# Cosine attention and token/channel mixer on one core: the first pair's loads, its k in two halves, and the sums of the second pair

## The chip, the core and the metric

The kernel runs on one core of one Trainium2 chip. The metric is the device time of one execution in microseconds (us). The engines are named as in the profile: PE (matrix multiplication), DVE (vector), ACT (scalar functions), POOL (general), SP (here it only issues DMAs). PEld is PE's loading of the stationary operand, and a "q" behind a name (SPq, ACTq, POOLq) is that engine's instruction queue when it issues DMAs.

## The reference

Eight batches, twelve heads, 448 tokens, head size 64; the mixer has d_model 768, d_tok 256 and d_ch 1536.

```python
q_n = q / (norm(q, axis=-1) + 1e-6)
k_n = k / (norm(k, axis=-1) + 1e-6)
scores = q_n @ k_n.T / tau                   # per batch and head
attn = softmax(scores)
x = (attn @ v)  as (batch, 448, 768)
h = relu(x.T @ w_tok1) @ w_tok2              # mixes the 448 tokens
u = x + h.T
out = u + relu(u @ w_ch1) @ w_ch2            # mixes the 768 channels
```

## The kernel before

**The unit of work is a pair of heads.** Twelve heads make NPAIR = 6 pairs a batch, and the 48 pairs of all batches are numbered i = 0 to 47. The 448 tokens lie as 112 partitions with 4 chunks each (SC = 112, NCH = 4), so a tile of q, k or v of a pair is 112 x 512 numbers in fp32, 224 KB, and each partition's part of one head is one contiguous run.

**The steps of a pair**, with the helper that records each one. `load_qk` and `load_v` issue the loads: q and v from SP's queue, k of pairs 0 to 2 from ACT's (L101 to L137). `square` squares q (a = 1) or k (a = 0), on ACT or POOL. `sums` adds up the squares over the head size, on DVE (L263). `norms` takes the square root as Ln and Exp on ACT (L276, L277), and, called again with `dve=True`, adds epsilon and takes the reciprocal on DVE (L273, L274). `scale` multiplies q or k by that, with a cast to fp16 into `kq` (L292), q on DVE and k on POOL for the first pairs. `tpose` turns the scaled chunks on PE into the PSUM tile `pst` and copies them on DVE to `qk` (L316, L318). `score(i, c)` multiplies chunk c of k with all of q on PE (L339), and ACT takes the exponential into `pt` (L340). `pv_wide` and `pv` multiply by v, which `cast_v` has cast on POOL (L216). `tok1` and `tok2` are the token mixer; `tok2` needs w_tok2 in the order that `place_w2` (POOL, L188) makes out of `w2n`, which `weights_tok2` loads from POOL's queue (L185). The channel mixer (`m_ch1`, L449, and `m_ch2`, L465) runs batch by batch behind it, as units from a queue that are put between the steps of later pairs.

**The order is written out by hand.** Under `tc.manual_schedule()` every engine runs its instructions in the order in which the helpers are called, and waits where an operand isn't there yet. Ahead of the loop stands a prologue for pairs 0 to 2 (L528 to L581), then a loop over i = 1 to 5 without the channel mixer, one written-out step for i = 6, and the loop for i = 7 to 47 with the channel mixer's units between the steps. In the loop's step i = 1 POOL runs `scale(2, 0)`, `cast_v(1)`, `square(4, 0)` and then `place_w2`, and step i = 2 begins with both scalings of pair 3 on POOL.

**DMA completions** are counted on eight semaphores that SP's and ACT's DMAs take in turn; a DMA that takes a semaphore again waits in its queue until the DMA eight places earlier has landed. SP's queue runs far ahead in this way. Its load of v of pair 4 also waits for `cast_v(0)`, since there are four buffers for v.

**Filler.** `warm(n)` records n matmuls of the identity that nobody reads (L330): 40 at the start, 3 and 5 around the turning of pair 0, later 8, 6 and 10.

Of the kernel before, what the change touches and what calls it, by code (L numbers as in the profile page):

```python
# [7 lines left out]
FP32 = mybir.dt.float32  # L8
FP16 = mybir.dt.float16
AF = mybir.ActivationFunctionType  # L10
ALU = mybir.AluOpType
AXX = mybir.AxisListType

ACT_SET_LN_EXP = 6


def _bcast_free(ap: bass.AP, n: int) -> bass.AP:
    new_ap = list(ap.ap) + [[0, n]]
    return bass.AP(tensor=ap.tensor, offset=ap.offset, ap=new_ap)
# [3 lines left out]
def kernel(  # L23
# [12 lines left out]
    nc = tc.nc  # L36

    B, H, S, E = q.shape
# [3 lines left out]
    SC = 112  # L42
    NCH = S // SC
# [22 lines left out]
    QS = 2 * NCH  # L66
# [17 lines left out]
    qkv = ctx.enter_context(tc.tile_pool(name="qkv", bufs=7))  # L84
# [4 lines left out]
    ps = ctx.enter_context(tc.tile_pool(name="ps", bufs=2, space=bass.MemoryType.PSUM))  # L89
    ps2 = ctx.enter_context(tc.tile_pool(name="ps2", bufs=3, space=bass.MemoryType.PSUM))  # L90

    half = {}
    pipe = {}
# [3 lines left out]

    def old(i):
        return i < OLD

    def load_rows(i, nm, src, bufs):  # L101
        h0 = 2 * (i % NPAIR)
        if old(i):
            t = qkv.tile([SC, QS, E], FP32, name=f"{nm}f_{i}", tag=f"{nm}f", bufs=bufs)
            (nc.scalar if nm == "k" and i < 3 else nc.sync).dma_start(
                out=t[:].rearrange("p (g c) e -> p g (c e)", g=2),
                in_=src[h0:h0 + 2].rearrange("g (p c) e -> p g (c e)", c=NCH))
            return t
        t = qkv.tile([128, 2 * KC, E], FP32, name=f"{nm}f_{i}", tag=f"{nm}f", bufs=bufs)
        nc.sync.dma_start(out=t[:].rearrange("p (g c) e -> p g (c e)", g=2),  # L110
                          in_=src[h0:h0 + 2, 0:128 * KC].rearrange("g (p c) e -> p g (c e)", c=KC))
        return t
# [9 lines left out]
    def load_qk(i):  # L122
        b, h0 = i // NPAIR, 2 * (i % NPAIR)
        n = i // HP
        half.setdefault(n, {})
        st = pipe[i] = {}
        st["q"] = qkv.tile([SC, QS, E], FP32, name=f"qf_{i}", tag="qf")
        nc.sync.dma_start(out=st["q"][:].rearrange("p (g c) e -> p g (c e)", g=2),
                          in_=q[b, h0:h0 + 2].rearrange("g (p c) e -> p g (c e)", c=NCH))
        st["k"] = load_rows(i, "k", k[b], 7)  # L130
        if not old(i) and "kr" not in half[n]:
            half[n]["kr"] = load_rest(i, "k", k[b])
# [51 lines left out]
    def weights_tok2():  # L184
        nc.gpsimd.dma_start(out=w2n[:], in_=moe_w_tok2.rearrange("(tt p) s -> p tt s", p=128))  # L185
# [16 lines left out]
    kqs = [cst.tile([128, 2, NCH, 2, E], FP16, name=f"kq{i}") for i in range(4)]  # L202
# [20 lines left out]
    def lay(i):  # L223
        n = QS if old(i) else KS
        return (slice(0, n), slice(n, n + QS)), (SC if old(i) else 128, SC)
# [25 lines left out]
    def sums_of(i):  # L251
        n, col, w = (-1 - i, 0, 1) if i < SINGLE else (i // HP, i % HP, HP)
        h = half.setdefault(n, {})
        if "ssq" not in h:
            tag = "" if w > 1 else "1"
            h["ssq"] = nrm.tile([128, w, 2 * QS], FP32, name=f"ssq_{i}", tag="ssq" + tag, bufs=4)
            h["rn"] = nrm.tile([128, w, 2 * QS], FP32, name=f"rn_{i}", tag="rn" + tag, bufs=4)
        return h, col

    def sums(i, a0=0, a1=2):  # L260
        n, sl = some(i, a0, a1)
        h, col = sums_of(i)
        nc.vector.tensor_reduce(out=h["ssq"][0:n, col, sl], in_=pipe[i]["sq"][0:n, sl],  # L263
                                axis=AXX.X, op=ALU.add)

    def norms(i0, i1, a0=0, a1=2, dve=False, act=False):
        h, col = sums_of(i0)
        n, sl = some(i0, a0, a1)
        ssq = h["ssq"][0:n, col:col + i1 - i0, sl]
        rn = h["rn"][0:n, col:col + i1 - i0, sl]  # L270
        ne = nes[i0 % 3][0:n, sl]
        if dve:
            nc.vector.tensor_reduce(out=rn[:, 0], in_=ne, axis=AXX.X, op=ALU.add)  # L273
            nc.vector.reciprocal(out=rn, in_=rn)  # L274
            return
        nc.scalar.activation(out=rn, in_=ssq, func=AF.Ln, bias=tiny[0:n])  # L276
        nc.scalar.activation(out=rn if act else ne[:, :, 0], in_=rn if act else rn[:, 0], func=AF.Exp, scale=0.5)  # L277
        if act:
            nc.scalar.activation(out=rn, in_=rn, func=AF.Ln, bias=eps[0:n])
            nc.scalar.activation(out=rn, in_=rn, func=AF.Exp, scale=-1.0)  # L280

    def scale(i, a, eng=None):
        st = pipe[i]
        eng = eng or nc.gpsimd
        sl, np_ = lay(i)
        if "kq16" not in st:
            st["kq16"] = kqs[i % 4]
        kq, p = st["kq16"], np_[a]
        h, col = sums_of(i)
        rn = h["rn"][:, col, sl[a]]  # L290
        n = KC if a == 0 and not old(i) else NCH
        eng.tensor_tensor(out=kq[0:p, a, 0:n].rearrange("p c g e -> p g c e"),  # L292
                          in0=st["kq"[a]][:].rearrange("p (g c) e -> p g c e", g=2),
                          in1=_bcast_free(rn[0:p, 0:2 * n].rearrange("p (g c) -> p g c", g=2), E), op=ALU.mult)
        if n == KC:
            if i < OLD + 4:
                eng.memset(kq[:, 0, KC].rearrange("p g e -> p (g e)"), 0.0)
            for g in range(2):
                p = slice(64 * g, 64 * g + 64)
                eng.tensor_scalar(out=kq[p, 0, KC, g], in0=half[i // HP]["kr"][p, i % HP],  # L300
                                  scalar1=rn[p, 2 * KC:KS], scalar2=1.0, op0=ALU.mult, op1=ALU.mult)
# [2 lines left out]
        scale(i, 0)  # L304
        scale(i, 1)

    def tpose(i, a0=0, a1=2):
        st = pipe[i]
        n = SC if old(i) else 128
        if "qk" not in st:  # L310
            qk = att.tile([128, 2 * NCH * 128], FP16, name=f"qk_{i}", tag="qk")
            st["qk"] = qk[:, 0:2 * NCH * n].rearrange("p (a c s) -> p a c s", a=2, c=NCH)
        pst = ps.tile([128, a1 - a0, NCH, n], FP16, name=f"pst_{i}_{a0}", tag="b")
        for a in range(a0, a1):
            for c in range(NCH):
                nc.tensor.transpose(pst[:, a - a0, c, :], st["kq16"][:n, a, c].rearrange("p g e -> p (g e)"),  # L316
                                    id16[:n, :n])
        nc.vector.tensor_copy(out=st["qk"][:, a0:a1], in_=pst[:])  # L318

    def tpose_dma(i):  # L320
        st = pipe[i]
# [5 lines left out]
    def warm(n, wide=False):  # L327
        w = (ps2 if wide else ps).tile([128, 128], FP32, name=f"warm{len(pipe)}_{n}", tag="s" if wide else "b")
        for _ in range(n):
            nc.tensor.matmul(w[:], id16[:], id16[:], start=True, stop=True)  # L330

    def score(i, c):
        n = SC if old(i) else 128
        qk = pipe[i]["qk"].rearrange("p a c s -> p (a c s)")
        qm = pipe[i]["qk"][:, 1, :, 0:SC]
        psS = ps2.tile([128, 2, 512], FP32, name=f"psS_{i}_{c}", tag="s")
        for hh in range(2):
            hb = slice(hh * 64, hh * 64 + 64)
            nc.tensor.matmul(psS[:, hh, 0:S], qk[hb, c * n:c * n + 128], qm[hb], start=True, stop=True)  # L339
        nc.scalar.activation(out=pts[i % 2][0:n, 2 * S * c:2 * S * (c + 1)].rearrange("p (h s) -> p h s", h=2),  # L340
                             in_=psS[0:n, :, 0:S], func=AF.Exp, scale=inv_tau)
# [183 lines left out]
    SU_AT = {15: [18, 19]}  # L525

    with tc.manual_schedule():
        for i in range(3):  # L528
            load_qk(i)
        load_v(0)  # L530
        load_qk(3)
        load_v(1)
# [1 line left out]
        load_v(2)  # L534
        load_qk(5)
        load_v(3)
        nc.scalar.add_instruction(mybir.InstLoadActFuncSet(
            name=nc.get_next_instruction_name(), act_func_set_id=ACT_SET_LN_EXP,
            ins=[], outs=[]))
        weights_tok1()  # L540

        square(0, 1, act=True)
# [1 line left out]
        sums(0, 1, 2)  # L544
        norms(0, 1, 1, 2)
        sums(0, 0, 1)
        norms(0, 1, 1, 2, dve=True)
        norms(0, 1, 0, 1)
        scale(0, 1, nc.vector)
        norms(0, 1, 0, 1, dve=True)  # L550
        scale(0, 0)
        square(1, 1, act=True)
        square(1, 0, act=True)
        square(2, 1, act=True)
        warm(40, True)
        sums(1)
        norms(1, 2)
        tpose(0, 1, 2)
        warm(3, True)
        tpose(0, 0, 1)  # L560
        warm(5, True)
        square(2, 0)
        weights_tok2()
        score(0, 0)
        score(0, 1)
        norms(1, 2, dve=True)
        scale(1, 0)
        scale(1, 1, nc.vector)
        sums(2)
        norms(2, 3)  # L570
        cast_v(0)
# [44 lines left out]
        i = NPAIR  # L616
# [53 lines left out]
        for i in range(NPAIR + 1, NP_ALL):  # L670
            b, pj = i // NPAIR, i % NPAIR
# [83 lines left out]
```

## Time and profile before

| | |
|---|---|
| median of 13 runs | 392.16 us (390.09 to 395.57) |
| the profiled execution | 390.8 us, its span 389.0 us, granted PE clock 0.995 of full |
| busy of the span: PE, DVE, ACT, POOL | 372.2, 209.0, 224.5, 237.2 us |
| PE busy from 0 to 40 us, and from 110 to 380 us | 32.3 of 40.0 us, 268.3 of 270.0 us |
| ACT and POOL busy from 18.4 to 40 us | 21.23 and 21.55 of 21.6 us |
| first square on ACT, first score on PE, first exponential on ACT | 4.59, 10.11, 10.71 us |

The span is the time from the first to the last instruction; the execution's own time is 1.8 us longer. The profile shows one execution, which lay 1.36 us below the median of the runs. The first 40 us are the stage in which no channel mixer runs: PE has gaps there, and ACT and POOL have none from 18.4 us on. From 110 us PE is busy for all but 0.6% of the time.

### The profile page before, as it was taken

The page shows a single profiled execution, that of the slowest core. Times are in us where ns is not written, and L with a number is a line of the kernel's source. Part 1 is how long each engine was busy: PE and PEld are TensorE (multiplying, and loading weights), DVE is VectorE, ACT ScalarE, POOL GpSimd, SP SyncE. Part 2 cuts the span into 40 slices and gives each one's busy share as a digit, 9 for nine tenths or more (in the row PEclk, how much of TensorE's full clock was granted, in tenths as well). Part 3 has the DMA queues.
Part 4 walks back from the last instruction along what each step waited for, and adds up shares of the span by engine and source line. Part 5 has one row for each costly group of instructions (what it writes and reads, how often), then busy time and mean ns, then how long its engine had stood idle before and what let it go on. Part 6 is the DMA issues. An engine that isn't in the chain of part 4 may idle for free.

```text
span 389.0 us, 10129 instructions
## 1 busy us (share of the span) xinstructions
PE 372.2 (96%) x4100; PEld 241.5 (62%) x4100; DVE 209.0 (54%) x457; ACT 224.5 (58%) x378; POOL 237.2 (61%) x384
## 2 busy tenths in 40 slices
PE   5889899999999999999999999999999999999995
PEld 5566566666557666666656666667656666565563
DVE  7789766776535673556535674456534553241031
ACT  5999687855575537745575537755574546501500
POOL 8899978897787674948577684847785540000000
PEclk9899999999999999999999999999999999999999
DMA  8999999999798698867797799888998392023023
GB/s 209 250 240 211 245 250 206 194 195 205 192 229 177 160 214 186 189 147 152 180 204 175 179 205 199 183 158 147 181 236 133 75 179 69 13 56 96 0 74 91
DMA packets 117055, 65.00 MB, mean 167 GB/s; under 512 B 74896, under 2 KB 113424, under 8 KB 117008
## 3 DMA queue, kind: packets, MB, share of 16 engines
q1 hardware_dynamic: 112112, 58.41, 70.6%
q0 software_dynamic: 4080, 5.21, 7.8%
q10 hardware_dynamic: 816, 0.73, 0.7%
q8 instruction: 32, 0.52, 0.6%
q14 instruction: 15, 0.12, 0.1%
HBM read 43.45 MB, written 11.01 MB: 140 GB/s over the span
## 4 chain that ended last, share of the span: by engine, by line
PE 80%; DMA 8%; POOL 6%; DVE 3%; issue 1%; SPq 1%; ACT 1%; POOLq 0%; ACTq 0%
PE psG L449 27%; PE psF L465 26%; PE psO L378 9%; PE psS L339 6%; PE psU L423 4%; PE psR L409 4%; DMA ut<-u 3%; POOL sq L240 2%; DMA w2n<-in_moe_w_tok_dram 2%; POOL kq L292 2%; PE psQ L346 2%; PE psO L361 1%; DMA qk<-kq 1%; DMA qf<-in_q_dram 1%; DVE ost L469 1%
## 5 line engine op out<-in xcount | busy, mean ns | idle before, releaser
L340 ACT ACTIVATE pt<-psS 128x896 f16<-128x896 f32 (+1 forms) x156 | 132.5, 916 | 53.1 <-PE psS L339 53.1
L449 PE MATMUL psG<-ut,wc1t 128*128 128x448 f16 x576 | 116.8, 352 | 0.5 <-DMA ut<-u 0.4
L465 PE MATMUL psF<-wc2t,gt 128*128 128x384 f16 (+2 forms) x684 | 116.2, 323 | 0.0
L465 PEld LDWEIGHTS <-gt 128*128 128x128 f16 x684 | 64.2, 98 | 38.0
L452 ACT ACTIVATE gt<-psG 128x448 f16<-128x448 f32 x96 | 51.5, 542 | 60.0 <-PE psG L449 60.0
L449 PEld LDWEIGHTS <-wc1t 128*128 128x128 f16 x576 | 53.9, 98 | 45.1 <-issue 0.9
L292 POOL TENSOR_TENSOR kq<-kf,rn 128x384 f16<-128x384 f32 (+1 forms) x48 | 42.9, 895 | 50.3 <-ACT rn L280 44.3
L469 DVE TENSOR_TENSOR ost<-psF,u 128x384 f32<-128x384 f32 (+2 forms) x65 | 35.6, 548 | 62.8 <-PE psF L465 60.2
L263 DVE TENSOR_REDUCE ssq<-sq 128x15 f32<-128x960 f32 (+2 forms) x49 | 55.7, 1140 | 4.5 <-ACT sq L238 3.7
L412 DVE TENSOR_SCALAR rt<-psR 128x256 f16<-128x256 f32 x48 | 20.2, 420 | 61.4 <-PE psR L409 61.3
L240 POOL TENSOR_TENSOR sq<-kf 128x384 f32<-128x384 f32 (+1 forms) x46 | 40.1, 872 | 17.0 <-DMA kf<-in_k_dram 15.5
L292 POOL TENSOR_TENSOR kq<-qf,rn 112x512 f16<-112x512 f32 x45 | 47.0, 1043 | 3.0
L339 PE MATMUL psS<-qk 64*128 64x448 f16 x312 | 42.1, 358 | 4.9 <-DVE qk L318 2.6
L378 PE MATMUL psO<-vt,pt 128*128 128x65 f16 (+1 forms) x1056 | 40.3, 193 | 0.2 <-DVE ut L440 0.2
L240 POOL TENSOR_TENSOR sq<-qf 112x512 f32<-112x512 f32 x39 | 40.5, 1039 | 0.0
L378 PEld LDWEIGHTS <-pt 128*128 128x128 f16 (+1 forms) x1056 | 35.2, 97 | 4.0 <-PE psS L339 1.0
L382 DVE TENSOR_TENSOR x<-psO,rec 128x256 f16<-128x256 f32 x84 | 35.6, 424 | 2.9
L426 DVE TENSOR_TENSOR u<-psU,x 128x512 f16<-128x512 f32 x48 | 33.0, 687 | 5.1 <-PE psU L423 3.6
L381 DVE RECIPROCAL rec<-psO 128x4 f32<-128x4 f32 x84 | 14.8, 176 | 29.5 <-PE psO L378 29.4
L409 PEld LDWEIGHTS <-w1t 128*128 128x128 f16 x384 | 24.9, 98 | 8.6 <-issue 1.5
L423 PEld LDWEIGHTS <-w2t 128*128 128x128 f16 x384 | 24.9, 98 | 7.8 <-issue 1.5
L423 PE MATMUL psU<-rt,w2t 128*128 128x128 f16 x384 | 29.3, 219 | 0.2 <-DVE qk L318 0.2
(58 smaller groups left out, 274.8 us busy)
## 6 DMA issues: line engine op xcount, KB each, us to landing
qf<-in_q_dram SPq DMA_DIRECT2D x48, 224.0 KB, 4.0
kf<-in_k_dram SPq DMA_DIRECT2D x36, 192.0 KB, 3.4
vf<-in_v_dram SPq DMA_DIRECT2D x36, 192.0 KB, 3.6
vf<-in_v_dram SPq DMA_DIRECT2D x12, 224.0 KB, 8.6
out_dram<-ost SPq DMA_DIRECT2D x8, 336.0 KB, 3.6
wc1t<-in_moe_w_ch_dram POOLq DMA_DIRECT2D x4, 576.0 KB, 10.4
wc2t<-in_moe_w_ch_dram POOLq DMA_DIRECT2D x2, 1152.0 KB, 12.2
out_dram<-ost SPq DMA_DIRECT2D x8, 288.0 KB, 3.1
```

The source lines that it names most:

```text
L240: nc.gpsimd.tensor_mul(out=dst, in0=src, in1=src)
L263: nc.vector.tensor_reduce(out=h["ssq"][0:n, col, sl], in_=pipe[i]["sq"][0:n, sl], axis=AXX.X, op=ALU.add)
L292: eng.tensor_tensor(out=kq[0:p, a, 0:n].rearrange("p c g e -> p g c e"), in0=st["kq"[a]][:].rearrange("p (g c) e -> p g c e", g=2), in1=_b ...
L339: nc.tensor.matmul(psS[:, hh, 0:S], qk[hb, c * n:c * n + 128], qm[hb], start=True, stop=True)
L340: nc.scalar.activation(out=pts[i % 2][0:n, 2 * S * c:2 * S * (c + 1)].rearrange("p (h s) -> p h s", h=2), in_=psS[0:n, :, 0:S], func=AF.Ex ...
L378: nc.tensor.matmul(psO[:, m, 0:E + 1], pts[i % 2][0:n, at:at + 128], vt[0:n, i % HP, nch * hh + c, 0:E + 1], start=(old(i) and c == 0), st ...
L409: nc.tensor.matmul(psR[:, tt], w1t[:, w1[m], tt * 128:(tt + 1) * 128], st["x"][:, m], start=(m == 0), stop=(m == 3))
L423: nc.tensor.matmul(psU[:, m], w2t[:, tt, lo:lo + 128], st["rt"][:, tt], start=(tt == 0), stop=(tt == TT - 1))
L449: nc.tensor.matmul(psG[:, 0:S], wc1t[:, dt, ct * 128:(ct + 1) * 128], ut[b][:, dt].rearrange("p m s -> p (m s)")[:, lo:lo + S], start=(dt ...
L452: nc.scalar.activation(out=gt[:, ct, (b % 2) * S:(b % 2 + 1) * S], in_=psG[:, 0:S], func=AF.Relu)
L465: nc.tensor.matmul(psF[:, 0:hi - lo], gt[:, ct, at:at + 128], wc2t[:, ct, lo:hi], start=(ct == 0), stop=(ct == CT - 1))
L469: nc.vector.tensor_tensor(out=o[p0:p1, lo:hi].rearrange("p (j e) -> p j e", e=128), in0=psF[p0:p1, 0:hi - lo].rearrange("p (j e) -> p j e" ...
```

## The change

The edits are all in the prologue, with two new helpers and two new arguments.

1. `load_first` loads q and k of pair 0 by heads: head 0 from SP's queue, head 1 from ACT's, q ahead of k on both. So far SP loaded q and ACT loaded k. The load of ACT's function table comes right behind these, ahead of the loads of pairs 1 and 2 instead of behind them.
2. k of pair 0 is scaled on POOL in two calls of two chunks each (`scale_part`) and turned in two calls of two chunks each (`tpose` with c0, c1). The second half is turned between `score(0, 0)` and `score(0, 1)`. Of the filler behind the turning, 5 matmuls become 3.
3. The sums of pair 1 are taken for q and k apart, and come behind the turning of q and between the halves of k, instead of ahead of the turning. `norms(1, 2)` moves from ahead of the turning to behind `score(0, 0)`, so that on ACT it stands behind the first exponential.
4. `weights_tok2()` moves from ahead of `score(0, 0)` to behind the scaling of pair 1; on POOL it then stands behind the scaling of k of pair 1.

```diff
+    def load_first(a, src):
+        t = qkv.tile([SC, QS, E], FP32, name=f"{a}f_0", tag=f"{a}f", bufs=7)
+        for g, eng in ((0, nc.sync), (1, nc.scalar)):
+            eng.dma_start(out=t[:, NCH * g:NCH * (g + 1)].rearrange("p c e -> p (c e)"),
+                          in_=src[0, g].rearrange("(p c) e -> p (c e)", c=NCH))
+        return t
...
+    def scale_part(i, a, c0, c1, eng):
+        st = pipe[i]
+        if "kq16" not in st:
+            st["kq16"] = kqs[i % 4]
+        h, col = sums_of(i)
+        rn = h["rn"][0:SC, col, lay(i)[0][a]]
+        eng.tensor_tensor(out=st["kq16"][0:SC, a, c0:c1].rearrange("p c g e -> p g c e"),
+                          in0=st["kq"[a]][:].rearrange("p (g c) e -> p g c e", g=2)[:, :, c0:c1],
+                          in1=_bcast_free(rn.rearrange("p (g c) -> p g c", g=2)[:, :, c0:c1], E), op=ALU.mult)
...
-    def tpose(i, a0=0, a1=2):
+    def tpose(i, a0=0, a1=2, c0=0, c1=NCH):
...
-        nc.vector.tensor_copy(out=st["qk"][:, a0:a1], in_=pst[:])
+        nc.vector.tensor_copy(out=st["qk"][:, a0:a1, c0:c1], in_=pst[:])
...
-        for i in range(3):
-            load_qk(i)
+        half[0] = {}
+        pipe[0] = {"q": load_first("q", q), "k": load_first("k", k)}
+        nc.scalar.add_instruction(mybir.InstLoadActFuncSet(
+            name=nc.get_next_instruction_name(), act_func_set_id=ACT_SET_LN_EXP,
+            ins=[], outs=[]))
+        load_qk(1)
+        load_qk(2)
         load_v(0)
...
-        nc.scalar.add_instruction(mybir.InstLoadActFuncSet(
-            name=nc.get_next_instruction_name(), act_func_set_id=ACT_SET_LN_EXP,
-            ins=[], outs=[]))
         weights_tok1()
...
+        norms(0, 1, 0, 1)
         norms(0, 1, 1, 2, dve=True)
-        norms(0, 1, 0, 1)
         scale(0, 1, nc.vector)
         norms(0, 1, 0, 1, dve=True)
-        scale(0, 0)
+        scale_part(0, 0, 0, 2, nc.gpsimd)
+        scale_part(0, 0, 2, NCH, nc.gpsimd)
...
         warm(40, True)
-        sums(1)
-        norms(1, 2)
         tpose(0, 1, 2)
         warm(3, True)
-        tpose(0, 0, 1)
-        warm(5, True)
+        sums(1, 1, 2)
+        tpose(0, 0, 1, 0, 2)
+        warm(3, True)
+        sums(1, 0, 1)
         square(2, 0)
-        weights_tok2()
         score(0, 0)
+        tpose(0, 0, 1, 2, NCH)
+        norms(1, 2)
         score(0, 1)
         norms(1, 2, dve=True)
         scale(1, 0)
         scale(1, 1, nc.vector)
+        weights_tok2()
         sums(2)
         norms(2, 3)
         cast_v(0)
```

## The prediction

> **What bounds the kernel now.** I read the page's shares first, then the busy time by stage, then the timeline of the first 20 us, and then the chain of waits there.
>
> ```profile
> 0.00:40.00 40.00, 32.30 (x472) 23.45 (x472) 32.66 (x74) 34.39 (x60) 36.76 (x60) 0.96 1.12 228
> 18.40:40.00 21.60, 19.34 (x328) 13.84 (x328) 18.59 (x40) 21.23 (x36) 21.55 (x25) 1.00 1.18 227
> 110.00:380.00 270.00, 268.27 (x2797) 171.60 (x2795) 129.60 (x276) 143.65 (x237) 141.61 (x236) 1.00 0.69 149
> ```
>
> The columns are stage, length, busy us of PE, PEld, DVE, ACT and POOL, granted clock, DMA share, GB/s. From 110 us PE is the bound and the change doesn't reach it, so the end moves by what the PE-bound stage's start moves. That start is set by ACT and POOL: from 18.4 to 40 us each idles under 0.4 us. A delay of either at 18 us can't be made up there. The prologue decides how late both get busy:
>
> ```profile
> 9.32 0.73 DVE L318 COPY qk<-pst 128x448 f16<-128x448 f16 x2
> 9.44 0.31 ACT L276 ACTIVATE rn<-ssq,tiny 112x16 f32<-112x16 f32 x1 [0.77 <-DVE ssq L263]
> 10.03 0.18 DVE L273 TENSOR_REDUCE rn<-ne 112x16 f32<-112x32 f32 x1
> 10.71 1.72 ACT L340 ACTIVATE pt<-psS 112x896 f16<-112x896 f32 x2 [0.71 <-PE psS L339]
> 11.15 1.21 DVE L263 TENSOR_REDUCE ssq<-sq 112x16 f32<-112x1024 f32 x1
> 12.39 0.31 ACT L276 ACTIVATE rn<-ssq,tiny 112x16 f32<-112x16 f32 x1
> 12.86 1.71 ACT L340 ACTIVATE pt<-psS 112x896 f16<-112x896 f32 x2
> 18.45 1.00 POOL L188 COPY w2t<-w2n 128x896 f16<-128x896 f16 x1 [1.11 <-DMA w2n<-in_moe_w_tok_dram]
> ```
>
> The columns are start and length in us, engine, line, operation. ACT takes pair 1's norms at 9.44, waits 0.71 us for the first score, and after 12.39 never rests again. POOL waits once more, 1.11 us at 18.45 for `w2n`. The chain of waits runs over the same load:
>
> ```profile
> 8.15 1.04 POOL kq L292
> 9.19 0.90 POOL sq L240
> 10.09 0.05 issue
> 10.14 8.26 DMA w2n<-in_moe_w_tok_dram
> 18.40 0.05 issue
> ```
>
> **The loads by heads.** Now q of pair 0 (224 KB, SP) lands at 4.51 and k (ACT's queue) before 4.95, both issued at 0.74. Between 2.75 and 3.75 us the windows show 356 to 377 GB/s, so with q's halves ahead of k's, 229 KB fewer lie before q's end: 0.61 us, and q lands at 3.90. But ACT's queue now holds k of pair 1 and k of pair 2 behind the table load and ahead of the first square, and the latter, the eighth DMA, waits for the first, q's head 0. An issue costs 0.43 to 0.49 us there (three in 1.46). So the first square starts at 3.90 + 0.46 + 0.08 = 4.44, 0.15 us earlier than 4.59. Bounds: 0.61 earlier if that issue delays nothing, 0.46 later if q lands no sooner. I take -0.15: the byte rate is a row of this stage. The table load (1.28 us) may hold back k of pair 1; its square at 7.54 isn't needed before its sums at 9.5, so up to 1.4 us stays covered.
>
> The row has 16 DMA engines at over 1.0 busy from 2.75 us on, whichever queue issued. The Trainium skill ("DMA: Bandwidth & Descriptors", section "Issuing engines are not separate DMA queues") says that queues of several engines share the same 16 DMA engines and only save issue time. By that rule the second queue brings nothing and only the new order does; and both queues were in use before. By a doubled rate, the reading that the rule speaks against, q would land another 0.3 us sooner.
>
> **k in halves and the moved sums** (times without the -0.15). Up to DVE's second reciprocal (ends 8.06) nothing changes.
> - DVE copies q at 8.22, as PE ended the turning at 8.18, until 8.59; sums of q of pair 1 (half of the pair at 5.26 that took 1.28: 0.64) until 9.25.
> - POOL scales half of k: 512 elements take 1.04, 384 take 0.82, 64 take 0.28, so 256 take about 0.59, 8.15 to 8.74; PE turns two chunks by 9.05, under DVE's sums. Two halves cost 0.14 us more on POOL than one call, hidden by its later wait.
> - DVE copies the half from 9.25: 448 elements take 0.365, 896 take 0.63, so 224 take 0.25, to 9.50. The first score starts at 9.56 instead of 10.11, the first exponential near 10.10 instead of 10.71: **0.6 us gained**.
> - The second sums end at 10.1, beside PE's score; the second half's turning and copy end near 10.5, and the second score is there at 11.2, before ACT is free. Two filler matmuls fewer save 0.2 us of PE in front of a wait: nothing.
>
> **What that costs.** `norms(1, 2)` now stands behind the exponential, which ends at 10.95 (half of 1.72 after 10.10). Its Ln and Exp end 0.55 later, so DVE's step that began at 10.03 begins at 11.48: **1.45 us later**. Queued behind it on DVE: reciprocal, scaling of q, then the sums of pair 2, which ended at 12.36 and now end at 13.81. ACT's norms of pair 2 wait for them and hold up the exponentials behind them. ACT's second exponential ends at 12.43 as before (the score comes earlier, the norms go between), then ACT idles 1.4 us. With the -0.15, everything of ACT from 12.39 on is 1.3 us late, and ACT has no gaps to make that up.
>
> POOL: the scaling of k of pair 1 waits for the same norms: from 11.98 instead of 10.96, to 13.1. Only then comes `w2n`'s issue, 13.1 instead of 10.14, 3.0 us later. `cast_v(0)` behind it goes from 12.09 to 13.9, and with it SP's load of v of pair 4, which waits for that cast, and all loads behind that: about 1.8 us later. q and k of pair 6, next there, were issued at 13.07 and 14.25 and squared at 27.15 and 26.32; 1.8 us later, and with 10.2 us to landing, the longest of these rows, they still land by 26.3. I cost it at nothing; a late one would show as POOL's wait on `kf`.
>
> When does `w2n` land? Its 8.26 us stand for waiting in line: the load of k of pair 5, issued at 9.30, had landed at 18.6, and v of pair 3, issued at 10.39, at 20.6, as SP's later issues that wait for them show:
>
> ```profile
> 18.63 0.31 SPq L128 DMA_DIRECT2D qf<-in_q_dram  x1
> 20.60 0.31 SPq L105 DMA_DIRECT2D kf<-in_k_dram  x1
> ```
>
> If landings follow issues, `w2n` now comes behind v of pair 3, with the same bytes before its end as that load had: 20.6, 2.2 us later. Bounds: the smallest load from POOL's queue (8 to 16 KB) took 6.4 us, giving 19.5 and +1.1, where ACT's +1.3 binds; the old 8.26 us give 21.36 and +2.95. I take +2.2. POOL's `place_w2` then starts 2.2 late and the scalings of pair 3 behind it as well, and ACT waits for those.
>
> **Sum.** POOL, without a gap until 51.3 us, carries +2.2 to the turning of pair 7 (38.11), behind which PE never waits over 0.4 us until 85. There PE waited 0.36 us at 44.71 for `ut`; that cover is used up: +1.84. The profiled execution becomes 390.8 + 1.84 = 392.6, and the median, 1.36 above it, 392.16 + 1.84 = **394.0**. About 0.5% (1.96 us) is what a measurement of this kernel can tell from no change, so this lies just inside it.
>
> **Rivals.**
> - *ACT alone binds* (0.17): `w2n` lands by 19.7, since SP's queue stands still until `cast_v(0)`, and fewer loads lie ahead. For it: that stop is 3.7 us long. Against: eight loads are in flight at 10.4. Then +1.3 - 0.36 to +1.3: 393.1 to 393.5.
> - *Faster* (0.14): the late norms cost nothing, because the sums of pair 2 are not what ACT waits for. The place is ACT's second Ln: if it starts by 12.39, the first exponential's 0.6 and the load's 0.15 remain, 391.4; if also the load's full 0.61 and the 0.81 us counts that `w2n`'s issue no longer takes ahead of POOL's scaling, -2.0: 390.1. For it: the two waits of 0.7 us on ACT before 10.71. Against: the order on DVE puts those sums behind the scaling that needs the norms. The chance is above what the rows alone give, as whole terms of the prologue may be missing here.
> - *The load does nothing it says* (0.08): q lands at 4.51 still, and the issue on ACT adds 0.54: +0.46 instead of -0.15, 1.84 + 0.61 gives 394.6, more if k of pair 1 is late.
> - *The clock closes again* (0.13). The granted clock was 0.51 between 10.0 and 13.4:
>
> ```profile
> 6.00:10.00 4.00, 1.23 (x17) 0.85 (x16) 3.70 (x9) 3.10 (x9) 3.28 (x5) 0.99 1.16 256
> 10.00:13.40 3.40, 3.29 (x24) 1.85 (x24) 2.53 (x6) 2.66 (x5) 3.39 (x5) 0.51 1.24 241
> 13.40:18.40 5.00, 4.03 (x68) 2.72 (x68) 4.44 (x10) 4.97 (x9) 3.39 (x4) 1.00 1.17 259
> ```
>
> PE, busy 1.23 of 4 us, lost half its clock for 3.4 us. With ACT's stop its work after 12.4 us is thinner; a second such stretch over work like 13.4 to 18.4 (81% busy: 2.75 of 3.4 us) would need 2.1 us more than the time has: +1.84 + 2.1 gives 396.1. The Trainium skill ("TensorE: Matmul & The Clock Gate", "What's actually happening") has a free-running window of about 3.4 us, with half the clock after an idle one; by it the first drop's place changes from run to run.
>
> **How the numbers follow.** The forecast (POOL waits for `w2n`) has 0.48; its bounds, 393.1 to 395.0, straddle 394.1, half each. ACT alone is within 0.5%. Of the faster case 0.09 lies beyond 0.5% and 0.05 within. The load and the clock are beyond it on the slow side. Faster 0.09, same 0.24 + 0.17 + 0.05 = 0.46, slower 0.24 + 0.08 + 0.13 = 0.45. The range leaves out most of the faster case and half of the clock's: 391.3 to 396.3.
>
> **What would show it.** Right: first score near 9.4 and first exponential near 9.95; ACT idle for over a microsecond ahead of its second pair of Ln and Exp, waiting for DVE's L263; `w2n` issued near 13, and POOL's wait ahead of its copy longer than 1.11 us, the copy starting at 20 to 21.5. Step by step wrong: a first square at 4.0 or at 5.0 (the load), a copy before 18.5 (the landing), ACT's second Ln by 12.5 (the norms). The whole is wrong if the turning of pair 7 starts before 38.1 us.

## The result, and the profile after

The changed kernel takes 395.11 us (median of 11 runs, 393.05 to 398.13) beside 391.15 us for the kernel before (48 runs in the same series, 389.75 to 395.57). The ratio is **1.0095, 95% interval 1.0068 to 1.0122**, or 3.7 us more, with 2.7 to 4.8 as the interval: slower, by more than the 0.5% that can be told from no change. The profiled execution took 396.1 us with a span of 394.3 us, 5.3 us more than the span before.

The busy time by stage comes first, as before: stage, length, busy us of PE, PEld, DVE, ACT and POOL, granted clock, DMA share, GB/s.

```profile
18.40:40.00 21.60, 17.17 (x287) 11.95 (x285) 18.93 (x39) 19.43 (x35) 18.96 (x22) 1.00 1.11 210
110.00:380.00 270.00, 268.26 (x2800) 171.45 (x2798) 129.53 (x275) 147.11 (x246) 146.86 (x244) 1.00 0.70 149
```

From 110 us PE is as full as before, so the loss lies ahead of it. From 18.4 to 40 us ACT and POOL were busy for 21.23 and 21.55 us before; now it is 19.43 and 18.96. They have got gaps, and the timeline (start, length, engine, line, what ended the idle time) shows where:

```profile
9.53 0.92 ACT L358 ACTIVATE pt<-psS 112x896 f16<-112x896 f32 x1 [0.79 <-PE psS L357]
11.58 1.44 POOL L248 TENSOR_TENSOR sq<-kf 112x512 f32<-112x512 f32 x1 [2.92 <-DMA kf<-in_k_dram]
13.96 0.81 POOL L193 DMA_DIRECT2D w2n<-in_moe_w_tok_dram  x1
14.30 0.31 ACT L284 ACTIVATE rn<-ssq,tiny 112x16 f32<-112x16 f32 x1 [2.61 <-DVE ssq L271]
16.07 3.42 DVE L310 TENSOR_TENSOR kq<-qf,rn 112x512 f16<-112x512 f32 x1
19.41 1.21 DVE L271 TENSOR_REDUCE ssq<-sq 112x16 f32<-112x1024 f32 x1
19.87 0.97 POOL L196 COPY w2t<-w2n 128x896 f16<-128x896 f16 x1 [0.93 <-DMA w2n<-in_moe_w_tok_dram]
20.65 0.31 ACT L284 ACTIVATE rn<-ssq,tiny 112x16 f32<-112x16 f32 x1 [2.02 <-DVE ssq L271]
21.92 1.04 POOL L310 TENSOR_TENSOR kq<-kf,rn 112x512 f16<-112x512 f32 x1 [1.08 <-DVE rn L282]
```

The line numbers are 8 to 18 higher than before: L310 is `scale`, L271 the sums, L284 the Ln, L248 the square on POOL. The first score (8.93) and the first exponential come 1.18 us earlier than before (10.11 and 10.71). Then everything slips. POOL waits 2.92 us for the load of k of pair 2, which cost it no wait before (its square stood at 9.16, right behind the scaling). ACT's Ln of pair 2 comes at 14.30 instead of 12.39. Then stands a row that no part of the prediction has: DVE's scaling of q of pair 2 takes **3.42 us**, where an instruction of this shape takes 0.69. The sums of pair 3 behind it start at 19.41 instead of 15.18, and ACT's Ln of pair 3 at 20.65 instead of 16.56: 4.09 us late. The turning of pair 7 is at 42.04 instead of 38.11 (+3.93) and the first `psG`, the channel mixer's first matmul, at 47.73 instead of 43.80 (+3.93).

`w2n` is the load on which the prediction put the loss. POOL waits 0.93 us for it at 19.87, less than the 1.11 us before, and then waits again, 1.08 us, for DVE's reciprocal. So the load isn't what binds here: an earlier landing would only have made the second wait longer. The chain of waits says so too: before, `w2n` filled it from 10.14 to 18.40. Now the chain runs over DVE.

```profile
16.07 1.00 DVE kq L310
17.08 2.33 issue
19.41 1.22 DVE ssq L271
```

"Issue" is time in which an engine waited for nothing that the profile shows. Its 2.33 us at 17.08 lie inside the 3.42 us of DVE's one instruction.

**What held it.** POOL's rows of the same time have no gap between them:

```profile
15.35 1.05 POOL L248 TENSOR_TENSOR sq<-kf 112x512 f32<-112x512 f32 x1
16.35 1.04 POOL L310 TENSOR_TENSOR kq<-kf,rn 112x512 f16<-112x512 f32 x1
17.34 0.60 POOL L224 CAST vt<-vf 112x512 f16<-112x512 f32 x1
17.91 1.03 POOL L248 TENSOR_TENSOR sq<-kf 112x512 f32<-112x512 f32 x1
```

They end at 18.94, and DVE's instruction ends at 19.49, 0.55 us later. It looks as if DVE could not begin while POOL had the next instruction ready. The kernel before shows the same encounter with the other outcome, in rows of its timeline:

```profile
14.20 0.69 DVE L292 TENSOR_TENSOR kq<-qf,rn 112x512 f16<-112x512 f32 x1
14.24 1.55 POOL L292 TENSOR_TENSOR kq<-kf,rn 112x512 f16<-112x512 f32 x1 [0.55 <-DVE rn L274]
```

There POOL was idle (0.55 us) and both engines waited for the same reciprocal of DVE. DVE went first and took its 0.69 us, and POOL's instruction took 1.55 us instead of 1.04: POOL was held for 0.51 us. What differs after the change is that `w2n`'s issue (0.81 us) now stands on POOL between the scaling of pair 1 and the square of k of pair 3. That square is therefore still running at 16.05, when the reciprocal is ready.

### The profile page after: what moved, and what is told of

Read it like the earlier page. It is cut to its first block, busy times and chain, and to the rows that moved or that the text cites. A ratio compares the mean times of both kernels' runs of the same rounds, so it can differ in the third digit from the quotient of the medians.

```text
span 394.3 us, 10131 instructions
## 1 busy us (share of the span) xinstructions
PE 373.7 (95%) x4098; PEld 242.1 (61%) x4098; DVE 211.9 (54%) x459; ACT 224.6 (57%) x378; POOL 237.4 (60%) x385
## 4 chain that ended last, share of the span: by engine, by line
PE 81%; ACT 5%; POOL 4%; DVE 3%; issue 2%; DMA 2%; SPq 1%; POOLq 0%; DVEq 0%
PE psG L467 27%; PE psF L483 26%; PE psO L396 9%; PE psS L357 6%; PE psU L441 5%; PE psR L427 4%; ACT pt L358 4%; PE psQ L364 2%; PE psO L379 1%; DMA kf<-in_k_dram 1%; POOL sq L248 1%; DVE ost L487 1%; DMA qk<-kq 1%; POOL w1t L189 1%; PE pst L334 1%
## 5 line engine op out<-in xcount | busy, mean ns | idle before, releaser
L310 POOL TENSOR_TENSOR kq<-kf,rn 128x384 f16<-128x384 f32 (+1 forms) x47 | 41.3, 879 | 49.5 <-ACT rn L288 44.0
L271 DVE TENSOR_REDUCE ssq<-sq 128x15 f32<-128x960 f32 (+2 forms) x50 | 55.8, 1120 | 4.2 <-ACT sq L246 2.9
L248 POOL TENSOR_TENSOR sq<-kf 128x384 f32<-128x384 f32 (+1 forms) x46 | 40.6, 882 | 23.9 <-DMA kf<-in_k_dram 23.8
L310 POOL TENSOR_TENSOR kq<-qf,rn 112x512 f16<-112x512 f32 x45 | 47.0, 1044 | 3.0
L248 POOL TENSOR_TENSOR sq<-qf 112x512 f32<-112x512 f32 x39 | 40.5, 1039 | 0.0
```

The costliest lines, as they stand in the source:

```text
L248: nc.gpsimd.tensor_mul(out=dst, in0=src, in1=src)
```

## The experiments

Three theories stood against each other.

- **A**: the loss is DVE's scaling of q of pair 2, held by POOL's work without a gap.
- **B**: the loss is the late landing of `w2n`.
- **C**: the loss is the order of the norms of pair 1, behind the first exponential.

The late load of k of pair 2, which stands behind the function table's load on ACT's queue, was a term of its own beside all three.

Every kernel was timed in five rounds beside the kernel before on the same chip: one chip for experiments 1 to 4, a second for 5 to 8, a third for 9 to 11. Ratios are to the kernel before in that series, with the 95% interval. The rows come from one execution of each kernel.

**1. The loads alone** (the kernel before with part 1 of the change).

```diff
-        for i in range(3):
-            load_qk(i)
+        half[0] = {}
+        pipe[0] = {"q": load_first("q", q), "k": load_first("k", k)}
+        # function table load
+        load_qk(1)
+        load_qk(2)
```

> The kernel before with part 1 of the change alone: pair 0 loaded by heads, table load ahead of the loads of pairs 1 and 2. Theory A (k of pair 2 lands late because its load is issued eighth; and a DVE scaling that meets POOL at work is held up): POOL's square of k of pair 2 starts at about 11.5 us instead of 9.16, sums of pair 2 at about 12.6, ACT's norms of pair 2 at about 13.8 instead of 12.39; 1.4 us slower than before, 3.5 if DVE's scaling of q of pair 2 is held up as well. Theory B (only the later w2n costs): POOL's copy of w2n waits, w2n issued about 12.6, 0 to 2 us slower. Theory C (only the later norms of pair 1 cost): this kernel has them in the old place, so it is 0.7 us faster.

Measured: **1.0038 (1.0009 to 1.0068)**. The first square starts at 3.62 and the first exponential at 10.20 instead of 10.71, but ACT's Ln of pair 2 is where it was (12.38) and so is the first `psG` (43.64). POOL waited 1.12 us for k of pair 2. A had expected that square at 11.5 and ACT's Ln at 13.8, and both are earlier. The 0.51 us gained at the first exponential are lost again in one row:

```profile
9.63 1.04 POOL L247 TENSOR_TENSOR sq<-kf 112x512 f32<-112x512 f32 x1 [1.12 <-DMA kf<-in_k_dram]
10.03 1.19 DVE L299 TENSOR_TENSOR kq<-qf,rn 112x512 f16<-112x512 f32 x1
```

DVE's scaling of q of pair 1 meets POOL's late square and takes 1.19 us instead of 0.69. It ends 0.55 us behind that square, as the long one ends 0.55 us behind POOL's last row. The next on POOL is `w2n`'s issue, and that doesn't hold DVE. Why the runs are a little slower than before, nothing in this profile's first 44 us says; the execution took 391.44 us, 1.6 less than the median of these runs.

**2. All the rest, with the loads of before.**

```diff
-        half[0] = {}
-        pipe[0] = {"q": load_first("q", q), "k": load_first("k", k)}
-        # function table load
-        load_qk(1)
-        load_qk(2)
+        for i in range(3):
+            load_qk(i)
...
+        # function table load
         weights_tok1()
```

> The changed kernel with the loads of before: parts 2 to 4 alone. Theory A: k of pair 2 lands at 8.3 as before, POOL's square of it is not late; norms of pair 2 start at 13.8 because the norms of pair 1 stand behind the first exponential (1.4 late); DVE's scaling of q of pair 2 starts while POOL is at work and takes over 2 us instead of 0.69; 1.4 us slower than before without that hold-up, 3.5 with it. Theory B: POOL's wait for w2n is longer than 1.11 us and the time follows it. Theory C: 1.4 us slower.

Measured: **1.0074 (1.0049 to 1.0099)**. The scaling of q takes 3.41 us, POOL's square of k of pair 2 starts at 9.09 without a wait, ACT's Ln of pair 2 is at 13.61 and the first `psG` at 47.06. Most of the loss is here, without the late load.

**3. The changed kernel with k of pair 2 early**: only the function table's load goes back behind ACT's loads.

```diff
         pipe[0] = {"q": load_first("q", q), "k": load_first("k", k)}
-        # function table load
         load_qk(1)
...
+        # function table load
         weights_tok1()
```

> The changed kernel with the table load put back behind ACT's loads, by which k of pair 2 is issued about 2.2 us instead of 3.3 and without waiting for another load. Theory A: it lands near 8.5 instead of 11.5, POOL's square of it starts by 9.5, norms of pair 2 at about 13.3 instead of 14.30; 1 us faster than the changed kernel, and up to 3 us if DVE's scaling of q of pair 2 then falls where POOL rests. Theories B and C: at most 0.5 us faster than the changed kernel.

Measured: **1.0081 (1.0051 to 1.0110)**. POOL's square starts at 9.06, so the late load is gone, and ACT's Ln of pair 2 goes from 14.30 to 13.66. The scaling still takes 3.42 us and the first `psG` is at 47.13, 0.6 us earlier than in the changed kernel. As long as the hold-up stands, the late load is worth little: 0.14% (0.5 us) less than the changed kernel, within the noise of the two, where A had expected 1 us and B and C at most 0.5.

**4. The changed kernel with the scaling of q of pair 2 on POOL** instead of DVE, which takes away the meeting and leaves `w2n` and the norms where the change put them.

```diff
-                scale(2, 1, nc.vector)
+                scale(2, 1)
```

> The changed kernel with q of pair 2 scaled on POOL (1.04 us there) instead of DVE (3.42 us in the changed kernel's trace, 0.69 before). Theory A: sums of pair 3 start by 17.2 instead of 19.41, ACT's norms of pair 3 near 18.4 instead of 20.65, and the time is 1.5 to 2.2 us less than the changed kernel's 395.1. Theories B and C: the scaling on DVE has nothing to do with it, and POOL's extra 1.04 us leaves the time where it is or adds up to 1 us.

Measured: **1.0046 (1.0028 to 1.0063)**, about half the loss. The rows of the timeline:

```profile
17.47 1.22 DVE L271 TENSOR_REDUCE ssq<-sq 112x16 f32<-112x1024 f32 x1 [1.08 <-ACT sq L246]
17.69 1.04 POOL L310 TENSOR_TENSOR kq<-qf,rn 112x512 f16<-112x512 f32 x1
20.23 0.98 POOL L196 COPY w2t<-w2n 128x896 f16<-128x896 f16 x1
```

The sums of pair 3 start at 17.47 instead of 19.41, although POOL has 1.04 us more to do and k of pair 2 came still later here (POOL's square at 12.32). They run beside POOL's gap-less work in their usual 1.22 us: a sum on DVE isn't held, only the scaling is. `place_w2` starts at 20.23 without a wait for `w2n`, which speaks against B in this kernel.

**5. The kernel before with part 4 alone** (`weights_tok2` behind the scaling of pair 1).

```diff
-        weights_tok2()
         score(0, 0)
...
         scale(1, 1, nc.vector)
+        weights_tok2()
```

> The kernel before with part 4 alone: w2n issued behind the scaling of k of pair 1. Theory A (POOL without a gap holds up DVE's scaling of q of pair 2): the 0.81 us of the issue now fill POOL's gap before that scaling, so DVE's scaling at about 14.2 takes 3.4 us instead of 0.69, the sums of pair 3 start near 17.6 instead of 15.18, ACT's norms of pair 3 near 18.8 instead of 16.56: 2 us slower than before. Theory B (w2n lands late): DVE's scaling keeps its 0.69 us, POOL waits longer than 1.11 us ahead of its copy, 1 to 2 us slower. Theory C (norms of pair 1): no change.

Measured: **1.0033 (1.0003 to 1.0064)**. One moved DMA issue makes the hold-up in a kernel that had none:

```profile
13.31 1.05 POOL L240 TENSOR_TENSOR sq<-kf 112x512 f32<-112x512 f32 x1
13.81 2.19 DVE L292 TENSOR_TENSOR kq<-qf,rn 112x512 f16<-112x512 f32 x1
15.31 1.16 POOL L216 CAST vt<-vf 112x512 f16<-112x512 f32 x1
19.91 0.99 POOL L188 COPY w2t<-w2n 128x896 f16<-128x896 f16 x1 [2.45 <-DMA w2n<-in_moe_w_tok_dram]
```

DVE is held for 1.50 us here and then goes ahead of the cast, which takes 1.16 us instead of 0.60. In this kernel `w2n` does come late, and POOL waits 2.45 us for it: so B may have a part when the rest of POOL is early enough to meet it, and this run doesn't part the two. The first `psG` is at 45.28.

**6. Experiment 3 with `w2n`'s issue back in its old place**, so that loads, halves, sums and norms are as in the change.

```diff
         square(2, 0)
+        weights_tok2()
         score(0, 0)
...
         scale(1, 1, nc.vector)
-        weights_tok2()
```

> The kernel with k of pair 2 early, and w2n issued in the old place, ahead of the scaling of pair 1; norms of pair 1 still behind the first exponential. Theory A: POOL rests between its square of k of pair 3 (ends near 15.0) and DVE's scaling near 15.4, so that takes 0.69 instead of 3.42 us; norms of pair 3 near 17.8 instead of 20.04; 2 us faster than with k of pair 2 early alone (393.5), about 1.2 slower than before, which is the delay of the norms of pair 2. Theory B: faster as well, but with DVE's scaling at 3.4 us and POOL's wait for w2n gone. Theory C: no faster.

Measured: **1.0003 (0.9982 to 1.0025)**, beside experiment 3's 1.0081. A had expected some 1.2 us more than before, from ACT's later Ln of pair 2 (13.53 here); the interval leaves at most 1.0. The meeting is that of before, with POOL's gap of 0.54 us and POOL as the one that is held:

```profile
15.33 0.69 DVE L310 TENSOR_TENSOR kq<-qf,rn 112x512 f16<-112x512 f32 x1
15.37 1.55 POOL L310 TENSOR_TENSOR kq<-kf,rn 112x512 f16<-112x512 f32 x1 [0.54 <-DVE rn L282]
```

**7. Experiment 3 with the norms of pair 1 ahead of the first exponential again.**

```diff
         sums(1, 0, 1)
+        norms(1, 2)
         square(2, 0)
...
-        norms(1, 2)
         score(0, 1)
```

> The kernel with k of pair 2 early, and the norms of pair 1 ahead of the first exponential again; w2n stays behind the scaling of pair 1. Theory A: norms of pair 2 start near 12.5 instead of 13.66, DVE's scaling of q of pair 2 still takes about 3.4 us because POOL has no gap; 1 us faster than with k of pair 2 early alone. Theory C: 1.5 to 2.5 us faster, back to the time before. Theory B: no change.

Measured: **1.0072 (1.0045 to 1.0099)**, not to be told from experiment 3. The scaling takes 3.42 us again. ACT's Ln of pair 2 gains 0.43 us (13.23; A had 12.5) and nothing comes of it, so C, which had 1.5 to 2.5 us here, falls. In this profile POOL waited 4.75 us for `w2n`, which lands by 22.65, and the first `psG` was at 48.95; the execution took 396.83 us, 3.5 more than the median of these runs.

**8. The kernel before with `w2n` issued first**, right behind w_tok1's loads on POOL's queue, to see whether an early landing is worth anything.

```diff
         weights_tok1()
+        weights_tok2()
...
         square(2, 0)
-        weights_tok2()
         score(0, 0)
```

> The kernel before with w2n issued right behind the loads of w_tok1, near 7.4 us instead of 10.14, ahead of the scaling of pair 0. Theory A: POOL's gap before DVE's scaling of q of pair 2 stays, POOL no longer waits 1.11 us ahead of its copy of w2n, and the kernel is 0 to 0.6 us faster than before, since ACT has no gap either. Theory B: 1.1 us faster.

Measured: **1.0046 (1.0023 to 1.0068)**, and the expectation missed. The experiment didn't do what it was for:

```profile
10.06 0.77 POOL L185 DMA_DIRECT2D w2n<-in_moe_w_tok_dram  x1 [2.59 <-DMA w1t<-in_moe_w_tok_dram]
```

The issue itself waited 2.59 us for a load of `w1t` from the same queue to land, with all of POOL behind it: the scaling of k of pair 0 started at 10.84 instead of 8.15. It says nothing about an early `w2n`.

**9. Experiment 6 with the norms of pair 1 ahead of the first exponential too.** What is left of the change is loads by heads, halves and split sums.

```diff
         sums(1, 0, 1)
+        norms(1, 2)
         square(2, 0)
...
-        norms(1, 2)
         score(0, 1)
```

> Edit: the version with k of pair 2 early and w2n's issue in its old place, and now also norms(1, 2) ahead of the first exponential again. What is left of the change: loads by heads, k of pair 0 in halves, sums of pair 1 split. Theory A (what costs is DVE's scaling of q of pair 2 held up by POOL work without a gap): the 0.8 us of w2n's issue stay between the sums' step and that scaling, so it takes about 0.7 us, not 3.4, first psG 45.0 to 45.5 us; ACT's Ln of pair 2 near 12.7 to 13.2 instead of 13.53, and the time between 0.8 us below that of the version without this edit (ratio to before 1.0003) and equal to it: ratio 0.998 to 1.000. Theory C (the order of the norms is worth over a microsecond once the hold-up is gone): ratio 0.997 or below, first psG at 44.2 or earlier. If the hold-up comes back (scaling 2.2 us or more), 1.003 to 1.008.

Measured: **1.0005 (0.9987 to 1.0023)**, 390.94 us beside 390.74. The interval holds what A said (0.998 to 1.000), and C's 0.997 or below lies outside it, though the first `psG` is where C had it (by 44.2). The profile is earlier than A said (the first `psG` at 43.9, where 45.0 to 45.5 was expected and experiment 6 had 45.5), without a gain in time: of these 1.6 us the two intervals together leave open about 1.0. The profile shows why the earlier first score is worth nothing in itself:

```profile
7.58 0.39 DVE L336 COPY qk<-pst 128x448 f16<-128x448 f16 x1
7.89 0.68 DVE L271 TENSOR_REDUCE ssq<-sq 112x8 f32<-112x512 f32 x1
8.60 0.28 DVE L336 COPY qk<-pst 128x224 f16<-128x224 f16 x1
8.79 0.68 DVE L271 TENSOR_REDUCE ssq<-sq 112x8 f32<-112x512 f32 x1
```

The first square starts at 3.97 instead of 4.59. But the two copies now stand ahead of the end of the second sums, which end at 9.47; before, one call ended at 9.41. The norms of pair 1 follow at 9.50 (9.44 before) and those of pair 2 at 12.45 (12.39 before). DVE's order passed the 0.62 us on to the first exponential (9.96 instead of 10.71) and nothing to the pairs behind.

**10. Experiment 1 with the function table's load behind ACT's loads**, as the kernel before has it.

```diff
-        # function table load
         load_qk(1)
...
+        # function table load
         weights_tok1()
```

> Edit: the kernel before with the loads of pair 0 by heads, and the function table's load behind all of ACT's loads, as the kernel before has it. In the version with the table load ahead the time was 1.0038 of before, though its first 44 us equalled before's in its profile. If that 0.4% came from the loads of pairs 1 and 2 behind the table load: ratio 1.000 to 1.001, and POOL's square of k of pair 2 starts without a wait on the load. If it came from the loads by heads themselves, or from the waits for qk between 80 and 110 us that vary between executions: 1.003 to 1.004 again.

Measured: **1.0003 (0.9972 to 1.0034)**; POOL's square of k of pair 2 starts at 9.03 with a wait of 0.23 us, and PE is busy for 28.98 of the 30 us from 80 to 110. Against experiment 1's 1.0038 this points to the place of the table's load, though the two intervals overlap.

**11. The changed kernel with `w2n`'s issue alone put back.**

```diff
         square(2, 0)
+        weights_tok2()
         score(0, 0)
...
         scale(1, 1, nc.vector)
-        weights_tok2()
```

> Edit: the changed kernel with weights_tok2 alone put back ahead of score(0, 0); the table load stays ahead of the loads of pairs 1 and 2. Theory A: the issue of 0.8 us on POOL stands ahead of the scaling of pair 1, so POOL's work behind it is again not without a gap at the moment at which DVE wants to scale q of pair 2; that scaling takes about 0.7 us; but k of pair 2 may come late (landing 9.5 to 12.3) and then costs up to 1 us. Ratio 1.000 to 1.003 and below that of the changed kernel (1.0095). Rival (the late load of k of pair 2 is half of the loss): ratio 1.005 or more with a scaling of 0.7 us.

Measured: **1.0039 (1.0015 to 1.0063)**. The scaling takes 0.69 us (15.36). What is left is the late load, here 1.77 us of waiting, and behind it a later issue of `w2n` (11.42) and a wait of 1.61 us for that:

```profile
10.44 1.04 POOL L248 TENSOR_TENSOR sq<-kf 112x512 f32<-112x512 f32 x1 [1.77 <-DMA kf<-in_k_dram]
20.12 0.99 POOL L196 COPY w2t<-w2n 128x896 f16<-128x896 f16 x1 [1.61 <-DMA w2n<-in_moe_w_tok_dram]
```

The ratio lies between A's 1.000 to 1.003 and the rival's 1.005: removing the hold-up takes away more than half of the loss. The rest goes with the place of the function table's load, ahead of the load of k of pair 2. That the late load carries it is argued and not shown: experiment 6 has its first `psG` only 0.24 us earlier (45.49) and no loss, and experiment 1 has a loss with the first `psG` of before.

**Together** (hold-up is the length of DVE's scaling of q of pair 2; the square is that of k of pair 2 on POOL):

| kernel | hold-up | square starts | first psG | ratio |
|---|---|---|---|---|
| before | 0.69 | 9.16 | 43.80 | 1 |
| after | 3.42 | 11.58 | 47.73 | 1.0095 |
| 3: after, table load late | 3.42 | 9.06 | 47.13 | 1.0081 |
| 4: after, q of pair 2 on POOL | none | 12.32 | 46.72 | 1.0046 |
| 11: after, `w2n` back | 0.69 | 10.44 | 45.7 | 1.0039 |
| 6: both 3 and 11 | 0.69 | 9.48 | 45.49 | 1.0003 |
| 9: 6, norms back | 0.69 | 8.67 | 43.9 | 1.0005 |

Between the changed kernel and the time of before lie two edits. `w2n`'s place is worth 0.56% (after to 11), 0.67% (7 to 9) and 0.78% (3 to 6), 2.2 to 3.1 us. The place of the function table's load is worth 0.14% (after to 3), 0.35% (1 to 10) and 0.36% (11 to 6), 0.5 to 1.4 us. These are differences of two ratios, most from two chips, and uncertain by 0.3 to 0.4% each way. So the first is shown, and the second, with one sign three times, is rough. Loads by heads, halves, sums and norms together are worth nothing that can be measured. No version beat the kernel before.

Putting `w2n`'s issue back also brings its data earlier, so these pairs alone don't part A from B. Experiment 4 does: `w2n` stays where the change put it, and half the loss goes. So do POOL's rows behind the copy: in the changed kernel and in experiments 2 and 3 POOL waits another 1.08, 1.58 and 1.10 us there for DVE's reciprocal, so an earlier `w2n` would not have let POOL's next scaling begin sooner.

The column of the first `psG` isn't the time: it comes from one execution. Those of the changed kernel and of experiments 3, 4 and 11 lay 1.0 to 2.4 us above the median of their runs, those of 6 and 9 within 0.2 us of it.

## Why the prediction was right or wrong

**The outcome.** 395.11 us lies in the range of 391.3 to 396.3, and 1.1 us above the forecast of 394.0. "Slower by over 0.5%" had 0.45, one point less than "within 0.5%". The growth was forecast as 1.84 us and is 3.7. That the time lies in the range is in part luck: the main term of the sum didn't bind, and the term that did wasn't in it. The forecast also stood on a median before of 392.16 us, where the series of the result has 391.15; with that it would have been 393.0, 2.1 us too low.

**The loads: the path right, the landing mis-sized.** The first square was put 0.15 us earlier, and came 0.68 earlier in the profile. As forecast, ACT's issue of k of pair 2 stands ahead of it and waits for a load of q:

```profile
3.48 0.33 ACTq L113 DMA_DIRECT2D kf<-in_k_dram  x1
```

It ends at 3.81, and the square starts 0.10 us later, at 3.91. The profile puts that wait down to a DVE memset that ended at 3.83; but in experiments 1, 4 and 11 the square also starts 0.11 us behind the end of that issue, at 3.62, 4.10 and 3.65, with the memset ending at 3.83 or 3.84 in each. So the issue does delay the square, as the prediction had it. What it had too small is the gain of the load. q's two halves landed 2.4 and 2.7 us after 0.74, by 3.44, which is 1.07 us ahead of 4.51 and not 0.61. The sum let the bytes begin when they did before, and they begin earlier: from 2.25 to 2.5 us the DMA engines moved 340 GB/s, where they moved 49 before. In the nine kernels with loads by heads it is 266 to 361 GB/s there, in the four others 45 to 131. Why isn't shown.

**k in halves and the norms: right, shifted by that.** The first exponential was put at 9.95 and came at 9.53. DVE's step of pair 1's norms was put 1.3 us late, and is at 10.92 instead of 10.03, 0.89 late: the difference is again 0.4 us. With k of pair 2 early (experiment 3) ACT's Ln of pair 2 is at 13.66, and the forecast was 1.3 us after 12.39, or 13.7.

**Missed on the same queue: k of pair 2.** The prediction saw that the table's load may hold back k of pair 1, and found it covered. It put k of pair 2, which stands behind that one, to the account of ACT's queue and not to its own reader. That reader, POOL's square, started at 11.58 instead of 9.16, and with it the scaling of k of pair 1 moved to 12.98 (forecast 11.98) and `w2n`'s issue to 13.96 (forecast 13.1).

**The step that failed: `w2n`.** Its landing was put at 20.6, with POOL carrying +2.2 us to the turning of pair 7. It had landed by 19.85, 5.9 us after its issue, below the 6.4 us that had served as the lower bound. The copy starts 1.42 us late instead of 2.2, and POOL then stands still for 1.08 us waiting for DVE, so that copy isn't the term of the sum. The right test was stated (a wait longer than 1.11 us ahead of the copy) and it fails: 0.93 us. The edit that moves the issue is the costly one all the same, but by the 0.81 us of POOL's time that it takes in its new place, and not by when the data land. Moving it 3 us later, the prediction counted what stands behind it in the queues and where it lands; it didn't ask which gap of POOL it fills. It had read that POOL waits once more behind 12.39, at 18.45; its timeline has another wait, the 0.55 us at 14.24, and that is the gap.

**The term that was missing: DVE held by POOL.** It is worth 2.73 us on DVE (3.42 less 0.69), and experiments 4 and 6 remove it in two different ways (11 as 6 does). Its sign was in the trace of before: 1.55 us in the row at 14.24 and 1.17 at 10.96, where the scaling of k otherwise takes 1.04 to 1.05, each time beside DVE's scaling of q. A duration that is half longer than its neighbours of the same shape is a sign to look at who runs beside it.

The Trainium skill has the rule ("SBUF — State Buffer", section "Who interferes with whom"): DVE and GpSimd (POOL here) share one pair of ports of SBUF, the memory on the chip that holds the tiles, under an exclusive lock, a DVE `tensor_tensor` with two SBUF inputs contends with GpSimd's reads, a `tensor_reduce` never does, and whoever issues first holds the other up for its whole instruction. The runs agree on who is held: in the kernel before it is POOL, by 0.51 us, after the change it is DVE, and the sums beside POOL's work in experiment 4 take their usual 1.22 us. In experiment 1 it is DVE for one instruction, as the rule says. The others differ from it on how long: in the changed kernel one instruction of POOL's would have cost DVE the 0.35 us that its square still had to run at 16.05, and DVE was held through that square and three more instructions.

**The rivals.** "ACT alone binds" named the right kind of place, since ACT does wait 2.61 us for its second Ln, but it ended at 393.5 us, with no instruction of DVE held. "Faster" fell at the place that it named itself: the second Ln comes at 14.30, not by 12.39. The clock's rival happened, and no cost of it shows. The four matmuls of a score at 16.17 took 0.93 us after the change, where those at 18.90 took 0.55, as did those at 13.89 before. Experiment 6 has the same 0.93 us at 15.43 and experiment 9 has 0.88 at 14.35, and both have the time of before: PE waits for other engines in this stage, so its slow stretch seems to lie under their work.

**The end.** The turning of pair 7 is 3.93 us late, and the first `psG` as late, so none of it was made up, and 3.7 us of it arrives. The profiled span grew by 5.3 us, 1.4 more than that. PE's busy time from 80 to 110 us is 25.90 instead of 27.95 us in this execution, waiting for the turned `qk` and for casts of v. Over the profiles of the other kernels that number goes from 26.30 (experiment 11) to 28.98 (experiment 10), with 26.66 in experiment 1 and 28.81 in experiment 9. Whether this wait follows from the prologue or only from one execution stays open.

## What to carry to other kernels

Before moving an instruction on POOL, even a DMA issue, look at the gap that it fills: a DVE operation that reads two operands from SBUF and used to slip into that gap may be held until POOL's next gap, and the price goes up to the length of POOL's whole uninterrupted run, not of one instruction. Compare the durations of equal shapes in the trace; one that is much longer than its neighbours may mark such a meeting, and which engine is held depends on a few tenths of a microsecond. A first result that comes earlier is worth only what the order of the engines behind it passes on, so follow it to the step at which the busy stage begins.

## What the hardware showed that was not expected

- A scaling on DVE that takes 0.69 us took 3.42 beside four instructions of POOL without a gap, in the change and in experiments 3 and 7 (3.41 in 2), 2.19 in experiment 5, where it got in after two, and 1.19 in experiment 1, where a DMA issue followed POOL's first. The loser doesn't simply take turns. What decides when it gets in was not tried. DVE's product of `psO` and `rec`, with one operand in PSUM, kept its 0.69 us at 16.55 in the kernel before, beside POOL's square at 16.31.
- An issue of a DMA on POOL can hold POOL's computing for 2.59 us, where an earlier load of its queue has not landed (experiment 8).
- A load that is issued 1.6 us later on the same queue (k of pair 2: the issues end at 3.80 instead of 2.20) landed 3.2 us later (11.52 instead of 8.32), and in the kernels with the function table's load ahead of it (the changed one and experiments 1, 4 and 11) POOL's start on it lay between 9.6 and 12.3 us. With the table's load behind it that start lay between 8.7 and 10.1 (experiment 8, where POOL itself was late, left out), and POOL still waited 1.33 us for it in experiment 7, so the table's load isn't all that sets it.
- The granted clock reads 1.00 from 13.4 to 18.4 us in the changed kernel, while the four matmuls at 16.17 took 0.93 us instead of 0.55. In experiment 11, with the same 0.93 us at 15.46, it reads 0.55. Durations of equal matmuls were the safer reading.
